# Attention groups of two blocks by four heads, with the results turned in 32x32 blocks on VectorE

## The chip, the cores and the metric

The kernel runs on one core of one Trainium2 chip. The time is device microseconds of one execution of the whole program; the median of a few runs is given. A profiled execution has a span of its own, from its first instruction to its last.

## What is computed

Local attention over 8 sequences of 576 tokens with 8 heads of 64, followed by a gated feed-forward layer over all 4608 tokens. Heads 0 to 3 see the 32 latest tokens ("plain"), heads 4 to 7 see 32 tokens at a distance of four ("strided").

```python
B, H, S, D = q.shape                     # 8, 8, 576, 64
scores = scale * np.matmul(q, k.transpose(0, 1, 3, 2))
mask_plain = (rel >= 0) & (rel < window)                                  # window = 32
mask_dil = (rel >= 0) & (rel < window * dilation) & (rel % dilation == 0) # dilation = 4
masks = np.stack([mask_plain if h < H // 2 else mask_dil for h in range(H)], axis=0)
scores = np.where(masks[None, :, :, :], scores, -1000000000.0)
scores = scores - np.max(scores, axis=-1, keepdims=True)
attn = np.exp(scores)
attn = attn / (np.sum(attn, axis=-1, keepdims=True) + 1e-09)
attn_out = np.matmul(attn, v)
x = np.ascontiguousarray(attn_out.transpose(0, 2, 1, 3)).reshape(B * S, H * D)   # 4608 x 512
g = x @ w_gate                                                            # 512 x 1536
silu = g * (1.0 / (1.0 + np.exp(-g)))
return silu * (x @ w_val) @ w_out                                         # 4608 x 512
```

## The kernel before

**The feed-forward layer sets the frame.** x is kept turned, with its 512 features on partitions (four blocks of 128, NK) and tokens along the free axis. Every fp32 number is split into a high and a low part that TensorE multiplies in one pass each, so a product is three matmuls. The first 1536 tokens go in four chunks of 384 (CH): for each chunk and each of 12 blocks f of the hidden layer, gv_mm issues 12 matmuls into bank_g and 12 into bank_v, and out_mm 12 into bank_o (L459, L496). The other 3072 tokens go in three chunks of 1024 by Strassen's seven products (products, L777, 128x512 each), whose inputs are made from the four quarters x32[a][t] (a: which half of the features, t: which 512 tokens). Weights come in 24 units at the start and pass through ScalarE, VectorE and GpSimd (w_one, stages E, T, B, H, L) before they can be used.

**Attention runs beside it in 46 packs.** In a block, 32 queries meet 64 keys. A pack (class Pack) holds 3 or 4 groups, and a group holds four blocks of 32 queries, one on each quarter of the 128 partitions, for two heads. Before the change a pack belongs to one pair of heads: the pair's two heads lie on the two halves of the rows of q and k (and side by side in the result), and the four quarters hold four blocks of queries, in a strided pack one for each residue modulo four. ORDER (2, 0, 3, 1) is the order of the pairs, and the order of x's feature blocks.

For pack m: scores (L354) multiplies q and k into the PSUM tile `two`; for packs 0 to 7 the mask is added by a matmul ahead, later by VectorE (L366). shift takes the maximum (L368) and subtracts it (L369); exps is the exponential on ScalarE (L374); turn_e turns the weights on TensorE (L378, one transpose of 128x128 per group), keys copies them to SBUF on ScalarE (L384); results multiplies them by v (L394), with a column of ones that gives the sums; norm adds epsilon, inverts and scales on VectorE (L403 to L405) into the buffer y.

y has queries on partitions, and x needs features there. turn_y turns each group of y on TensorE (L412) by one of two identities: a plain one, or one with its columns in another order, which puts strided queries back in the order of tokens. x_copies then takes the result from PSUM: in the chunks of 384 ScalarE makes the high part and VectorE the low part (L429, L430; in the opening L444, L448), later ScalarE copies into x32 (L438).

**What sets the order.** The opening (packs 0 to 3) is written out by hand in a string of steps: Q scores, S shift, X exps, T turn_e, K keys, A results, N norm, U turn_y, H and L the two parts of x, W a stage of the weights, Y idle matmuls. Afterwards a table of visits gives each pack two slots between the matmul groups of the layer: at A(m) the sums of pack m-1, the scores of m, norm of m-1, shift and exps of m; at B(m), three or more slots on, turn_y of m-1, turn_e and keys of m, x_copies of m-1. Within an engine a scheduler places the instructions. `two`, q and k, v, e, y and the turned weights have one buffer each after the opening.

## Time and profile before

| what | value |
|---|---|
| time, median of 3 runs | 947.46 us (946.64 to 948.33) |
| span of the profiled execution | 945.3 us |
| feed-forward matmuls in chunks of 384 | to about 383 us |
| the three chunks of 1024 | 383 to 572, 572 to 759, 759 to 945 us |
| last visit of a pack | about 735 us |

The span of the profiled execution lies 2.2 us below the median of the runs. In the profile PE is TensorE's matmuls, PEld its weight loads, DVE is VectorE, ACT ScalarE, POOL GpSimd, SP SyncE. A row of a group has its line, engine and operation, what it writes and reads, its count, the time during which any of it ran, the mean of one in ns, and the idle time before it. A row in order of time has its start and how long it lasted in us; at its end stands in brackets how long the engine had stood idle and what ended that. Matmuls overlap, so how far one group pushes the next back is read from start to start. A row of the waits has the engine and line that waited, for whom, the sum in us, how often, and the longest. A row of a stretch has its bounds, its length, the busy time of PE, PEld, DVE, ACT and POOL with their counts, the granted clock, the share of the DMA and its GB/s.

### The profile page before, as it was taken

What the parts mean: (1) busy time and instruction counts of PE and PEld (TensorE: products, weight loads), DVE (VectorE), ACT (ScalarE), POOL (GpSimd) and SP (SyncE); (2) the same over time, 40 slices, a digit from 0 to 9 for tenths busy, and PEclk for the clock granted to TensorE, in tenths of its full rate; (3) what the DMA queues carried; (4) which work ended last, traced back from release to release, by engine and by line L of the source; (5) the groups of instructions that cost most, each with busy time, mean ns of one, the idle gap of its engine ahead of it and who ended that gap; (6) DMA issues with size and microseconds to landing.
All of it is one profiled execution on the core that took longest, in us unless ns stands there. A gap on an engine that the chain in (4) does not pass through costs nothing.

```text
span 945.3 us, 21894 instructions
## 1 busy us (share of the span) xinstructions
PE 929.0 (98%) x9193; PEld 810.9 (86%) x9193; DVE 633.3 (67%) x1008; ACT 391.9 (41%) x687; POOL 345.9 (37%) x364
## 2 busy tenths in 40 slices
PE   7899999999999999999999999999999999999998
PEld 4799999999999999888888788888887888888886
DVE  4767566676677865666568984666689845656882
ACT  4885323233233334343344553343355523334352
POOL 0765421111111131224245672232257723344481
PEclk9999999999999999999999999999999999999999
DMA  9985156577767791776667678776764786655573
GB/s 371 330 282 202 36 200 204 189 235 238 237 196 236 244 324 39 226 245 205 227 205 258 202 241 260 229 235 199 254 203 162 232 256 192 198 185 176 177 249 107
DMA packets 75249, 205.25 MB, mean 217 GB/s; under 512 B 7568, under 2 KB 23824, under 8 KB 75152
## 3 DMA queue, kind: packets, MB, share of 16 engines
q0 software_dynamic: 27216, 99.10, 33.4%
q1 hardware_dynamic: 35696, 65.07, 19.3%
q10 hardware_dynamic: 12240, 39.70, 12.7%
q8 instruction: 72, 1.18, 0.5%
q14 instruction: 25, 0.20, 0.1%
HBM read 161.37 MB, written 42.47 MB: 216 GB/s over the span
## 4 chain that ended last, share of the span: by engine, by line
PE 91%; DVE 4%; DMA 2%; ACT 2%; issue 1%; ACTq 0%; DVEq 0%
PE bo L777 30%; PE bg L777 11%; PE bv L777 11%; PE bo L496 10%; PE bv L459 10%; PE bg L459 10%; PE two L394 3%; PE two L354 2%; PE two L378 2%; DVE at_float L740 2%; PE two L412 1%; DMA at_int<-w 1%; DMA at_float<-qkb 1%; ACT at_float32r L274 0%; DVE at_float L805 0%
## 5 line engine op out<-in xcount | busy, mean ns | idle before, releaser
L777 PE MATMUL bo<-at_float32r 128*128 128x512 f32 x1296 | 308.0, 391 | 0.0
L777 PEld LDWEIGHTS bo<-at_float32r 128*128 128x128 f32 x1296 | 242.1, 188 | 51.6 <-ACT at_float L503 0.2
L706 POOL DMA_DIRECT2D at_float32r<-pieces x189 | 103.5, 548 | 249.7 <-PE bo L777 147.0
L740 DVE TENSOR_TENSOR at_float<-bo,at_float 128x512 f32<-128x512 f32 x168 | 113.8, 686 | 109.6 <-ACT at_float L782 59.8
L488 POOL TENSOR_TENSOR at_float32r<-at_float,at_float32r 128x384 fp32r<-128x384 f32 x48 | 55.4, 1154 | 219.7 <-PE bo L496 179.7
L777 PE MATMUL bv<-at_float32r 128*128 128x512 f32 x486 | 129.7, 393 | 0.0
L777 PE MATMUL bg<-at_float32r 128*128 128x512 f32 x486 | 129.6, 393 | 0.0
L740 DVE TENSOR_TENSOR at_float32r<-at_float,at_float32r 128x512 fp32r<-128x512 f32 (+1 forms) x84 | 99.2, 1205 | 40.5 <-ACT at_float32r L767 24.9
L459 PE MATMUL bg<-at_float32r,at_float32r 128*128 128x384 f32 x576 | 110.9, 339 | 2.1 <-DVE at_float L473 1.3
L740 POOL TENSOR_TENSOR at_float32r<-at_float,at_float32r 128x512 fp32r<-128x512 f32 x63 | 96.4, 1532 | 44.7 <-ACT at_float32r L767 43.3
L459 PE MATMUL bv<-at_float32r,at_float32r 128*128 128x384 f32 x576 | 110.6, 339 | 0.0
L496 PE MATMUL bo<-at_float32r,at_float32r 128*128 128x384 f32 x576 | 110.1, 338 | 0.0
L777 PEld LDWEIGHTS bv<-at_float32r 128*128 128x128 f32 x486 | 90.1, 188 | 19.3
L777 PEld LDWEIGHTS bg<-at_float32r 128*128 128x128 f32 x486 | 90.2, 188 | 19.0 <-DVE at_float32r L740 0.2
L767 ACT CAST at_float32r<-at_float 128x512 fp32r<-128x512 f32 x126 | 76.2, 622 | 68.1 <-PE bv L777 23.2
L459 PEld LDWEIGHTS bg<-at_float32r,at_float32r 128*128 128x128 f32 x576 | 100.0, 188 | 3.8 <-POOL at_float32r L278 1.1
L496 PEld LDWEIGHTS bo<-at_float32r,at_float32r 128*128 128x128 f32 x576 | 100.2, 188 | 0.9
L459 PEld LDWEIGHTS bv<-at_float32r,at_float32r 128*128 128x128 f32 x576 | 100.0, 188 | 1.0 <-DVE at_float L478 0.3
L803 ACT ACTIVATE at_float<-at_float 128x512 f32<-128x512 f32 x72 | 45.6, 633 | 85.4 <-DVE at_float L740 85.2
L473 DVE SCALAR_TENSOR_TENSOR at_float<-at_float,bg 128x384 f32<-128x384 f32 x48 | 26.6, 553 | 76.7 <-ACT at_float L468 76.7
L782 ACT COPY at_float<-bg 128x512 f32<-128x512 f32 x63 | 36.9, 586 | 86.2 <-PE bg L777 86.1
L278 POOL TENSOR_TENSOR at_float32r<-at_int,at_float32r 128x768 fp32r<-128x768 f32 x24 | 45.8, 1916 | 41.5 <-ACT at_float32r L274 41.3
(80 smaller groups left out, 966.3 us busy)
## 6 DMA issues: line engine op xcount, KB each, us to landing
at_float32r<-pieces POOLq DMA_DIRECT2D x189, 512.0 KB, 4.5
pieces<-at_float32r SPq DMA_DIRECT2D x126, 256.0 KB, 4.8
at_int<-w SPq DMA_DIRECT2D x24, 768.0 KB, 6.9
at_float<-vb ACTq DMA_DIRECT2D x28, 390.0 KB, 4.6
at_float<-vb ACTq DMA_DIRECT2D x14, 520.0 KB, 5.5
at_float<-qkb ACTq DMA_DIRECT2D x14, 448.0 KB, 5.5
out<-at_float SPq DMA_DIRECT2D x24, 256.0 KB, 5.3
at_float<-qkb ACTq DMA_DIRECT2D x10, 544.0 KB, 6.7
```

The lines of the kernel that those rows point to most:

```text
L278: nc.gpsimd.tensor_tensor(out=lo, in0=wst.pop(u).bitcast(F32), in1=hi, op=ALU.subtract)
L394: nc.tensor.matmul(out=two[BQ * j:BQ * j + BQ, h, (D + 1) * g:(D + 1) * (g + 1)], lhsT=t[r, BQ * i:BQ * i + BQ], rhs=v[r, i, :], start=Tru ...
L459: nc.tensor.matmul(out=bank[:, :CH], lhsT=wcol(f, o, low), rhs=x[ORDER[j]], start=n == 0, stop=n == len(ops) - 1)
L473: last["h"] = nc.vector.scalar_tensor_tensor(out=t, in0=t, scalar=1.0, in1=bank_g[:, :CH], op0=ALU.add, op1=ALU.mult)
L488: nc.gpsimd.tensor_tensor(out=hl, in0=hst[i][0], in1=hst[i][1], op=ALU.subtract)
L496: nc.tensor.matmul(out=bank_o[j][:, :CH], lhsT=wcol(f, 2 * DM + P * j, low), rhs=x, start=f == 0 and low == 0 and x is hh, stop=f == NF - ...
L706: nc.gpsimd.dma_start(out=taken[asked], in_=pieces[asked % NPIECE])
L740: engine.tensor_tensor(out=out, in0=a, in1=b, op=op)
L767: nc.scalar.copy(out=o[:, 0], in_=src)
L777: nc.tensor.matmul(out=bank, lhsT=w, rhs=x, start=first and n == 0 and t in FRESH, stop=last and n == len(ops) - 1, skip_group_check=True)
L782: nc.scalar.copy(out=kept[KEPT[t]][r], in_=banks[0][r][:, :CS])
L803: nc.scalar.activation(out=f, in_=g, func=AF.Tanh, scale=0.5)
```

## The change

A group now holds, for two blocks of queries, all four plain or all four strided heads. The four quarters of the partitions hold the four heads, and the two halves of the rows hold the two blocks (i = 0, 1). A plain pack covers half of its tokens with each half of the rows; a strided pack covers two of the four residues, and a second pack (part) the other two. The count of packs (46) and of groups (152) stays, and so do the shapes of scores, turn_e and results.

With one head on each quarter, turning every 32x32 block of y by itself puts features on partitions and tokens along the free axis: quarter j then holds 32 features of head j, and y's two halves of features (c) lie side by side. turn_y becomes one VectorE transpose of the whole y, in place, or straight into x32 for a plain pack of the last three chunks. One feature block of x now holds half of the features of four heads; the rows of the gate and value weights are laid out to match on the host. x_hi and x_lo are indexed by plain or strided. The copies into x read y in SBUF. The second identity is no longer loaded; the table of masks has 16 groups instead of 12; q and k of plain packs have more columns, since each head's keys lie apart. Strided copies write every fourth column of x32, and each half of it is cleared once on GpSimd.

```diff
 def packs():
-    out = [Pack(c, p, CH * c, CH * c + CH) for c in range(NPLAIN) for p in ORDER]
+    out = []
+    for c in range(NPLAIN):
+        lo = CH * c
+        half = [Pack(c, 0, n, lo + CH // 2 * n, lo + CH // 2 * (n + 1)) for n in range(2)]
+        rest = [Pack(c, 1, n, lo, lo + CH) for n in range(2)]
+        out += half + rest if c == 0 else [rest[0], half[0], rest[1], half[1]]
...
     def norm(m, two, pool):
...
-        nc.vector.tensor_tensor(out=y.rearrange("q g h d -> q h g d"), in0=s[:, :, :, :D],
-                                in1=z.unsqueeze(3).broadcast_to([P, 2, ng, D]), op=ALU.mult)
+        nc.vector.tensor_tensor(out=y.rearrange("q (c i g d) -> q i g c d", c=2, i=2, g=ng),
+                                in0=s[:, :, :, :D].rearrange("q i g (c d) -> q i g c d", c=2),
+                                in1=z.unsqueeze(3).unsqueeze(4).broadcast_to([P, 2, ng, 2, D // 2]), op=ALU.mult)
...
-    def turn_y(m, bank):
-        for g in range(pk(m).ng):
-            nc.tensor.transpose(out=bank[:, P * g:P * g + P], in_=st[m]["y"][:, g].rearrange("q h d -> q (h d)"),
-                                identity=idents[:, pk(m).order])
+    def turn_y(m):
+
+        y = st[m]["y"]
+        out = y
+        if pk(m).chunk >= NPLAIN and not pk(m).strided:
+            t, o = divmod(pk(m).lo - T0 - 2 * CS * (pk(m).chunk - NPLAIN), CS)
+            n = 2 * BQ * pk(m).ng
+            out = x32[1][t][:, :, o:o + n]
+            y = y.rearrange("p (c t) -> p c t", c=2)
+        nc.vector.transpose(out=out, in_=y)
...
+    def x_copy(m, what):
+        c = pk(m).chunk
+        for first, o, n in x_runs(m):
+            src, xh, xl = x_views(m, first - CH * c, o, n, *(t[c % 2][pk(m).strided] for t in (x_hi, x_lo)))
+            if what == "hi":
+                nc.scalar.copy(out=xh, in_=src)
+            else:
+                nc.vector.tensor_tensor(out=xl, in0=src, in1=xh, op=ALU.subtract)
...
+                    if t not in clear:
+                        clear.add(t)
+                        nc.gpsimd.memset(x32[0][t], 0.0)
+                    src, dst = x_views(m, a, o, w, x32[0][t])
+                    nc.scalar.copy(out=dst, in_=src)
...
-        ops = [(j, 0, x) for j in range(NK) for x in (xh, xl)] + [(j, 1, xh) for j in range(NK)]
+        ops = [(j, 0, x) for j in KORDER for x in (xh, xl)] + [(j, 1, xh) for j in KORDER]
...
-        for what in ("Q0 Q1 Y2 S0 X0 T0 Y2 S1 K0 X1 A0 M0 W0 Q2 N0 T1 K1 S2 X2 Q3 W1 W0 S3 X3 A1 U0 N1 W2 T2 K2 H0 L0 W3 W4 "
-                     "T3 A2 K3 W1 U1 N2 A3 H1 L1 W0 W2 U2 N3 W3 H2 U3 L2 W4 H3 L3 W1 W0 W2 W1 W2 W3 W0 W0").split():
+        for what in ("Q0 Q1 Y2 S0 X0 T0 Y2 S1 K0 X1 A0 M0 W0 Q2 N0 T1 K1 S2 X2 Q3 U0 W1 H0 W0 S3 X3 A1 N1 L0 U1 W2 T2 K2 H1 L1 W3 W4 "
+                     "T3 A2 K3 W1 N2 U2 A3 H2 W0 L2 W2 N3 U3 W3 H3 L3 W4 W1 W0 W2 W1 W2 W3 W0 W0").split():
...
             if m < NPK:
                 shift(m, two, later, m < 8)
+            if m > 4:
+                turn_y(m - 1)
+            if m < NPK:
                 exps(m)
...
         elif what == "B":
-            if m > 4:
-                turn_y(m - 1, two[:, 0])
             if m < NPK:
                 turn_e(m, two[:, 1])
                 keys(m, two[:, 1], later)
             if m > 4:
-                x_copies(m - 1, two[:, 0])
+                x_copies(m - 1)
```

KORDER is (2, 3, 0, 1), the plain feature blocks first. Lines of the changed kernel that the rows below name: L388, L390 and L391 are the mask's addition, the maximum and the subtraction (before L366, L368, L369), L425 to L427 are norm (L403 to L405), L444 is the transpose of y, L400 is turn_e (L378), L499 and L536 are the matmuls of gv_mm and out_mm (L459, L496), L780, L845 and L846 are element-wise passes of the chunks of 1024 (L740, L805, L806). at_... are SBUF buffers.

TensorE at slot B of pack 23, in the last chunk of 384, before:

```order
L459 MATMUL bg<-at_384_float32r,at_1536_float32r 128x384 x12
L459 MATMUL bv<-at_384_float32r,at_1536_float32r 128x384 x12
L412 MATMUL two<-at_256_float_59,at_384_float_1071 128x128 x3
L378 MATMUL two<-at_256_float_59,at_512_float_691 128x128 x4
L496 MATMUL bo_490<-at_384_float32r,at_1536_float32r 128x384 x2
```

The same place after:

```order
L499 MATMUL bg<-at_768_float32r,at_1536_float32r 128x384 x12
L499 MATMUL bv<-at_768_float32r,at_1536_float32r 128x384 x12
L400 MATMUL two<-at_128_float_59,at_512_float_675 128x128 x4
L536 MATMUL bo_474<-at_384_float32r,at_1536_float32r 128x384 x2
```

The three turns of pack 22's results are gone from between the matmuls of the layer and turn_e; the rest keeps its order.

VectorE at slot A of pack 23, before:

```order
L403 TENSOR_SCALAR at_6_float_285<-two 128x6
L404 RECIPROCAL at_6_float_285<-at_6_float_285 128x6
L405 TENSOR_TENSOR at_384_float_1071<-two,at_6_float_285 128x2x3x64
L366 TENSOR_TENSOR at_512_float_691<-two,at_448_bfloat_58 128x2x4x64
L368 TENSOR_REDUCE at_8_float_2996<-at_512_float_691 128x8
L369 TENSOR_TENSOR at_512_float_691<-at_512_float_691,at_8_float_2996 128x2x4x64
```

The same place after:

```order
L425 TENSOR_SCALAR at_6_float_277<-two 128x6
L426 RECIPROCAL at_6_float_277<-at_6_float_277 128x6
L427 TENSOR_TENSOR at_384_float_1054<-two,at_6_float_277 128x6x2x32
L388 TENSOR_TENSOR at_512_float_675<-two,at_576_bfloat_58 128x2x4x64
L444 STREAM_TRANSPOSE at_384_float_1054<-at_384_float_1054 128x384
L390 TENSOR_REDUCE at_8_float_2958<-at_512_float_675 128x8
L391 TENSOR_TENSOR at_512_float_675<-at_512_float_675,at_8_float_2958 128x2x4x64
```

The transpose of pack 22's results stands between the mask's addition and the maximum of pack 23, ahead of the subtraction.

VectorE at slot A of pack 35, in the first chunk of 1024, where the scheduler puts passes of the layer in between, before, from the scaling of y to the subtraction:

```order
L405 TENSOR_TENSOR at_384_float_1071<-two,at_6_float_285 128x2x3x64
L366 TENSOR_TENSOR at_512_float_691<-two,at_448_bfloat_58 128x2x4x64
L740 TENSOR_TENSOR at_1024_float32r<-at_512_float_536,at_1024_float32r 128x512
L368 TENSOR_REDUCE at_8_float_2996<-at_512_float_691 128x8
L740 TENSOR_TENSOR at_1024_float32r<-at_512_float_4759,at_1024_float32r 128x512
L369 TENSOR_TENSOR at_512_float_691<-at_512_float_691,at_8_float_2996 128x2x4x64
```

The same place after:

```order
L427 TENSOR_TENSOR at_384_float_1054<-two,at_6_float_277 128x6x2x32
L388 TENSOR_TENSOR at_512_float_675<-two,at_576_bfloat_58 128x2x4x64
L444 STREAM_TRANSPOSE at_384_float_1054<-at_384_float_1054 128x384
L390 TENSOR_REDUCE at_8_float_2958<-at_512_float_675 128x8
L780 TENSOR_TENSOR at_1024_float32r<-at_512_float_520,at_1024_float32r 128x512
L391 TENSOR_TENSOR at_512_float_675<-at_512_float_675,at_8_float_2958 128x2x4x64
```

The transpose comes in, and one of the two passes with two SBUF operands that stood ahead of the subtraction no longer stands there.

More of the change, by code (lines that the diff above doesn't have):

```diff
@@ L434, in x_copies @@
                 first -= T0 + 2 * CS * (c - NPLAIN)
                 while n:
[L436 to L448 removed]
+                    t, a = divmod(first, CS)
```

235 lines of the change are left out of this document (121 added, 114 removed).

## The prediction

> **What bounds the kernel now.** I read the engine table and the granted clock first, then the chain of waits, then the list of who waited for whom, then the order of time around single visits.
>
> ```profile
> span 945.3 us, 21894 instructions
> PE 929.0 (98%) x9193; PEld 810.9 (86%) x9193; DVE 633.3 (67%) x1008; ACT 391.9 (41%) x687; POOL 345.9 (37%) x364
> ...
> PEclk9999999999999999999999999999999999999999
> ...
> PE 91%; DVE 4%; DMA 2%; ACT 2%; issue 1%; ACTq 0%; DVEq 0%
> ```
>
> TensorE is busy for 98% of the span at full granted clock, and the chain that ended last runs over it for 91%. So what is taken off TensorE's own stream is worth its time, as long as nothing that TensorE then waits for comes later. The same chain by line shows what turning the results costs it (the row is cut at the view's width):
>
> ```profile
> by line: PE bo L777 30.2%; PE bg L777 10.9%; PE bv L777 10.7%; PE bo L496 10.4%; PE bv L459 10.3%; PE bg L459 10.1%; PE two L394 2.8%; PE two L354 2.4%; PE two L378 1.6%; DVE at_float L740 1.6%; PE two L412 1.5%; issue 1.0%; DMA at_int<-w 1
> PE two L378 <- ACT at_float L374: 3.6, 3, 1.6
> ```
>
> L412 (turn_y) is 1.5% of 945.3 us, 14.2 us, and all of that line goes. The second row is TensorE's list of waits: the visits' other transpose, L378 (turn_e), waited three times, 3.6 us in all, for ScalarE's exponentials (L374). The change touches exactly that place: it takes work off TensorE just ahead of L378, and puts work on VectorE ahead of the exponentials.
>
> **The change, step by step.**
>
> *TensorE loses the turns of the results.* There are 152 groups of 128 columns before and after, so scores, weighted sums and turn_e keep their counts; only L412 falls away: 140 transposes in the visits, 12 in the opening.
>
> ```profile
> L412 PE MATMUL two<-at_float,at_float 128*128 128x128 f32 x140 | 22.1, 272 | 0.0
> 244.31 2.24 PE L459 MATMUL bv<-at_float32r,at_float32r 128*128 128x384 f32 x12
> 246.39 0.49 PE L412 MATMUL two<-at_float,at_float 128*128 128x128 f32 x3
> 246.72 0.60 PE L378 MATMUL two<-at_float,at_float 128*128 128x128 f32 x4
> ...
> 257.00 2.25 PE L459 MATMUL bg<-at_float32r,at_float32r 128*128 128x384 f32 x12
> 259.08 0.60 PE L412 MATMUL two<-at_float,at_float 128*128 128x128 f32 x4
> 259.52 0.49 PE L378 MATMUL two<-at_float,at_float 128*128 128x128 f32 x3
> ```
>
> The mean of 272 ns and the 22.1 us of the group overlap with neighbours, so I take start to start: three transposes push L378 back by 246.72 - 246.39 = 0.33 us, four by 259.52 - 259.08 = 0.44, 0.11 each. 140 x 0.11 = **15.4 us**. The chain's 14.2 agrees once the two visits below are left out in which L412 only shortened a wait. L378 then follows the matmuls directly, as L412 did.
>
> *VectorE gains 46 transposes.* One per pack, of 384 or 512 columns from SBUF to SBUF. No such operation is in the trace. The nearest rows are the passes of the same size over one operand in SBUF, and above them the pass over two SBUF operands that GpSimd often holds up:
>
> ```profile
> L368 DVE TENSOR_REDUCE at_float<-at_float 128x6 f32<-128x384 f32 x26 | 14.3, 551 | 0.7
> L368 DVE TENSOR_REDUCE at_float<-at_float 128x8 f32<-128x512 f32 x12 | 8.2, 683 | 0.3
> L740 DVE TENSOR_TENSOR at_float32r<-at_float,at_float32r 128x512 fp32r<-128x512 f32 x63 | 71.0, 1148 | 24.9 <-ACT at_float32r L767 24.9
> ```
>
> I bound the price between nothing (where the queue has a gap before the next operation anyway) and 1.15 us, and take the rows it is nearest to, one operand and as many columns: 0.55 us for 384 and 0.69 for 512, some 27 us over a queue that has 945 - 633 = 312 us free. What counts is its place: the order of VectorE shows it in every visit between the mask's addition (or the maximum) and the last subtraction, so it stands ahead of the exponentials, and what is queued behind it there is the maximum, the subtraction, then ScalarE's exponentials and TensorE's L378. Each visit's exponentials come later by the transpose of the pack before, d, and TensorE arrives earlier by the turns it no longer does, u (0.33 or 0.44). With s the spare time of before (start of L378 less the end of the exponentials, less the 0.05 us from 521.93 to 521.98 in a visit that waited), d + u - s is given back where it is positive. The rows of the visits with the least to spare, and of the first with enough:
>
> ```profile
> 76.26 0.63 ACT L374 ACTIVATE at_float<-at_float 128x512 f32<-128x512 f32 x1 [0.58 <-DVE at_float L369]
> 77.35 0.60 PE L378 MATMUL two<-at_float,at_float 128*128 128x128 f32 x4
> ...
> 92.07 0.53 ACT L374 ACTIVATE at_float<-at_float 128x384 f32<-128x384 f32 x1
> 92.66 0.54 PE L378 MATMUL two<-at_float,at_float 128*128 128x128 f32 x3
> ...
> 321.02 0.63 ACT L374 ACTIVATE at_float<-at_float 128x512 f32<-128x512 f32 x1 [3.50 <-DVE at_float L369]
> 322.38 0.60 PE L378 MATMUL two<-at_float,at_float 128*128 128x128 f32 x4
> ...
> 344.19 0.64 ACT L374 ACTIVATE at_float<-at_float 128x512 f32<-128x512 f32 x1 [2.58 <-DVE at_float L369]
> 345.71 0.60 PE L378 MATMUL two<-at_float,at_float 128*128 128x128 f32 x4
> ...
> 521.30 0.63 ACT L374 ACTIVATE at_float<-at_float 128x512 f32<-128x512 f32 x1 [2.87 <-DVE at_float L369]
> 521.98 0.66 PE L378 MATMUL two<-at_float,at_float 128*128 128x128 f32 x4 [1.62 <-ACT at_float L374]
> ...
> 538.43 0.53 ACT L374 ACTIVATE at_float<-at_float 128x384 f32<-128x384 f32 x1 [3.93 <-DVE at_float L369]
> 539.56 0.49 PE L378 MATMUL two<-at_float,at_float 128*128 128x128 f32 x3
> ...
> 717.76 0.66 PE L378 MATMUL two<-at_float,at_float 128*128 128x128 f32 x4 [1.16 <-ACT at_float L374]
> ...
> 196.84 0.52 ACT L374 ACTIVATE at_float<-at_float 128x384 f32<-128x384 f32 x1
> 199.01 0.49 PE L378 MATMUL two<-at_float,at_float 128*128 128x128 f32 x3
> ```
>
> Pack 6 (77.35): s = 77.35 - 76.89 - 0.05 = 0.41, so 0.55 + 0.33 - 0.41 = 0.47 us. Pack 7 (92.66): s = 0.01, 0.69 + 0.44 - 0.01 = 1.12. Pack 23 (322.38): s = 0.68, 0.20. Pack 25 (345.71): s = 0.83, 0.05. Pack 36 (539.56): s = 0.55, 0.69 + 0.44 - 0.55 = 0.58. Packs 35 (521.98) and 45 (717.76) waited already, s = 0: 0.88 each. Pack 13 (199.01) has 1.60, more than 0.88, and so have the other visits behind the opening (pack 4 has no results to turn). Together **4.2 us given back**. With a transpose at nothing it is still 1.1 (packs 7, 35, 45); at 1.15 us (and 1.53 for 512 columns) the same seven visits give 8.9. At packs 35 and 45 the estimate is loosest: the chain to the subtraction is stretched there by passes between two SBUF operands, and the new order has one of those fewer ahead of the subtraction.
>
> ```profile
> 517.49 2.55 POOL L740 TENSOR_TENSOR at_float32r<-at_float,at_float32r 128x512 fp32r<-128x512 f32 x2
> 518.00 2.59 DVE L740 TENSOR_TENSOR at_float32r<-at_float,at_float32r 128x512 fp32r<-128x512 f32 x1
> ```
>
> Such a pass takes 2.59 us while GpSimd works on the same kind. The Trainium skill, SBUF — State Buffer, section "Who interferes with whom", says that a VectorE instruction with two SBUF inputs contends with GpSimd's reads and one with a single input does not; this pair of rows agrees with the first half, and no row of before shows the second. By that rule the transpose is never held, and the price stays near 0.55 beside GpSimd too.
>
> *Copies of x.* They now read y in SBUF. On ScalarE the plain packs of the last three chunks lose theirs (the transpose writes x directly), the strided packs of chunk 1 get two instead of one. On VectorE the 18 subtractions for the low part get two SBUF operands, so one may rise from about 0.55 towards 2.59 us. They stand behind the exponentials, where TensorE has no wait in the list, and the visits of those chunks after pack 7 have at least 1.6 us: 0, and at most 1. Two clears of 128x1024 on GpSimd come ahead of low-part passes for the second product, which follow several matmul groups later: 0. y has one buffer, and the next visit's scaling must now wait for ScalarE's copy rather than for TensorE's turn; the copy is queued at B, before the next visit's sums that precede the scaling: 0.
>
> *The opening.* It is run by loads and ScalarE, not by TensorE:
>
> ```profile
> 0.00:28.00 28.00, 20.94 (x455) 14.15 (x455) 15.06 (x33) 14.41 (x25) 3.69 (x6) 0.94 0.96 375
> 16.49 0.92 ACT L235 ACTIVATE at_int<-at_int 128x768 f32<-128x768 f32 x1 [2.07 <-DMA at_int<-w]
> ```
>
> TensorE is busy 21 of the first 28 us, so its 12 turns bring nothing, and VectorE (15 of 28) holds four more passes of 0.55. The DMA is 96% busy at 375 GB/s; ahead of the second weight unit, for which ScalarE waits at 16.49, stand 96 KB more (96 columns more of q and k, 48 KB, for each of packs 1 and 3; 64 KB more of masks, 64 KB less of identities): 98304 bytes at 375 GB/s, 0.26 us. The first gate matmuls now need both plain packs, but the last of them still follow pack 3's results. I take **0.3 us lost**, between 1 gained and 1.5 lost.
>
> **The sum:** 945.3 - 15.4 + 4.2 + 0.3 = 934.4 us of span. The median shown is 947.46, 2.2 above the profiled span; I let those 2.2 stand for what lies around it: **936.6 us**.
>
> The Trainium skill speaks against this price: VectorE: DVE Perf Modes, section "The three transpose paths", gives 311 ns for a VectorE transpose of 128x128 in bf16, which read as 128 columns is an estimate of 0.93 us for 384; the visits would give back 7.2 us and the sum would be 939.6. No run here shows it yet.
>
> **The rivals.**
>
> *The transpose costs about twice the row I took.* For: nothing in the trace shows such an operation, so the upper row is as open as the lower. Against: the upper row owes its length to GpSimd, and the passes over one operand agree among themselves (551 and 683 ns). At 1.15 us: 945.3 - 15.4 + 8.9 + 0.3 + 2.2 = 941.3.
>
> *Nothing is given back.* The order after is the scheduler's, and at packs 35 and 45 it drops a pass that could be held 2.59 us. Then the old waits shrink as much as packs 6, 7 and 36 lose: 945.3 - 15.4 + 0.3 + 2.2 = 932.4.
>
> *The time isn't recovered, because every L378 waits for its exponentials.* Each turn's 0.11 us would become a wait: 947.5. Against it stand three waits in 46 visits.
>
> *Slower: VectorE's queue becomes the bound of every visit.* With the same subtraction over all 42 visits, 14 of them wait once the transpose takes 1.75 us, and they give back 15.1, which is the point of no gain; at 2.0 us it is 19.3, and the time 945.3 - 15.4 + 19.3 + 0.3 + 2.2 = 951.7. For: a held pass took 2.59 us. Against: three times the price of the nearest row, for one operand.
>
> **How the numbers follow.** Forecast 0.62, twice the price 0.16, nothing given back 0.09, time not recovered 0.05, slower 0.08. The range goes from 932 (nothing given back) to 942.5 (twice the price, and 1.2 us more in the opening). A measurement of this kernel can tell 0.2%, 1.9 us, from no change: faster 0.62 + 0.16 + 0.09 = 0.87, same 0.05, slower 0.08.
>
> **What would show it.** Right: no transposes of y on TensorE and L378 right behind the matmuls; transposes on VectorE near 550 and 690 ns; TensorE's waits for the exponentials at some 3.6 + 4.2 = 8 us, seven times, at packs 6, 7, 35, 36 and 45 above all; matmul groups as long as before; the first 28 us within 1.5. Wrong: transposes over 1.1 us; waits for exponentials in many visits; TensorE waiting for copies of x, for low parts or for weights, which it doesn't now.

## The result, and the profile after

| kernel | median, us | lowest to highest | ratio to before, 95% |
|---|---|---|---|
| before (4 runs) | 947.6 | 946.64 to 948.33 | |
| changed (4 runs) | 937.27 | 935.84 to 937.64 | 0.9891 [0.9877, 0.9905] |

The change makes the kernel 1.1% faster, 10.3 us. The profiled execution has a span of 934.1 us, 11.2 less than before. Its engine table and, behind the dots, the chain that ended last by engine:

```profile
span 934.1 us, 21615 instructions
...
PE 913.8 (98%) x9041; PEld 795.7 (85%) x9041; DVE 661.9 (71%) x1056; ACT 393.5 (42%) x671; POOL 337.8 (36%) x366
...
PE 90%; DVE 6%; DMA 2%; ACT 2%; issue 1%; SPq 0%; ACTq 0%; DVEq 0%
```

TensorE loses 15.2 us of busy time and 152 matmuls; VectorE gains 28.6 us and stays free for 29% of the span. The chain is still TensorE's, but VectorE's share of it went from 4 to 6%. The groups by line and shape give the price of the new operation (busy time of the group, then the mean of one in ns):

```profile
L444 DVE STREAM_TRANSPOSE at_float<-at_float 128x384 f32<-128x384 f32 x32 | 18.2, 568 | 0.1
L444 DVE STREAM_TRANSPOSE at_float<-at_float 128x512 f32<-128x512 f32 x14 | 9.8, 701 | 0.0
```

Three rows of TensorE's list of waits (line, what it waited for, total, times, longest) hold most of what is given back of the turns:

```profile
PE two L400 <- ACT at_float L396: 4.4, 4, 2.5
PE fs L400 <- ACT at_float L396: 3.2, 1, 3.2
PE bv L499 <- ACT at_float32r L290: 2.7, 1, 2.7
```

The first row is the visits (L400 is turn_e, L396 the exponentials): 4.4 us where before had 3.6. The second is the opening's last pack, the third is new: TensorE waits for the high part of a weight unit (L290). By visit, the waits for exponentials, read from the order of time:

| pack | 4 | 25 | 35 | 36 | 45 | 6, 7, 23 |
|---|---|---|---|---|---|---|
| before, us | 0.78 | 0 | 1.62 | 0 | 1.16 | 0 |
| after, us | 0 | 1.27 | 0.33 | 2.53 | 0.32 | 0 |

Where the 11.2 us arise is seen by comparing when the same matmul of the layer starts (start after less start before; n counts the layer's matmuls ahead of it):

| n, layer matmuls ahead (start before) | 70 (38.3) | 144 (55.5) | 936 (215.1) | 1512 (335.6) | 1584 (351.7) | 2268 (522.4) | 2376 (549.5) | last (940.9) |
|---|---|---|---|---|---|---|---|---|
| difference, us | +2.8 | +1.8 | -2.0 | -5.6 | -3.9 | -8.9 | -6.6 | -11.2 |

The opening loses 2.8 us by matmul 70, and 1.0 of them is back by matmul 144, mostly pack 4's wait of 0.78 us, which is gone. From there each visit gains 0.327 us (three turns) or 0.437 (four), and two places give back: the visit of pack 25 (between matmuls 1512 and 1584) and that of pack 36 (2268 to 2376). These are the two visits in the order of time, VectorE's rows ahead of TensorE's L400:

```profile
337.85 0.80 ACT L487 COPY at_float<-at_float 128x64 f32<-128x64 f32 x2 [3.27 <-DVE at_float L444]
338.45 0.52 ACT L508 ACTIVATE at_float<-bg 128x384 f32<-128x384 f32 x1
338.68 1.23 DVE L780 TENSOR_TENSOR at_float<-at_float,at_float 128x1024 f32<-128x1024 f32 x1 [0.30 <-ACT at_float L487]
339.83 0.68 DVE L391 TENSOR_TENSOR at_float<-at_float,at_float 128x512 f32<-128x512 f32 x1
...
341.57 0.66 PE L400 MATMUL two<-at_float,at_float 128*128 128x128 f32 x4 [1.27 <-ACT at_float L396]
...
529.98 0.70 DVE L444 STREAM_TRANSPOSE at_float<-at_float 128x512 f32<-128x512 f32 x1
530.61 0.51 DVE L390 TENSOR_REDUCE at_float<-at_float 128x6 f32<-128x384 f32 x1
531.04 0.68 DVE L780 TENSOR_TENSOR at_float<-bo,at_float 128x512 f32<-128x512 f32 x1
531.64 0.55 DVE L391 TENSOR_TENSOR at_float<-at_float,at_float 128x384 f32<-128x384 f32 x1
...
532.85 0.55 PE L400 MATMUL two<-at_float,at_float 128*128 128x128 f32 x3 [2.53 <-ACT at_float L396]
```

At pack 25 a sum of the layer (L780) stands ahead of the subtraction (L391) and itself waits 0.30 us for ScalarE's copy of x (L487). At pack 36 the transpose is one of several passes between 528.5 us, when the sums of the pack before begin, and the subtraction.

In the opening the second weight unit comes late. VectorE, ScalarE and TensorE after:

```profile
21.23 0.58 DVE L444 STREAM_TRANSPOSE at_float<-at_float 128x384 f32<-128x384 f32 x1
21.85 0.89 ACT L466 CAST at_float32r<-at_float 128x384 fp32r<-128x384 f32 x1 [0.62 <-DVE at_float L444]
22.77 0.85 DVE L468 TENSOR_TENSOR at_float32r<-at_float,at_float32r 128x384 fp32r<-128x384 f32 x1 [0.96 <-ACT at_float32r L466]
23.54 0.95 DVE L279 SCALAR_TENSOR_TENSOR at_int<-at_int 128x768 int32<-128x768 int32 x1
24.52 0.83 ACT L290 CAST at_float32r<-at_int 128x768 fp32r<-128x768 f32 x1 [1.09 <-DVE at_int L279]
25.40 1.18 PE L499 MATMUL bv<-at_float32r,at_float32r 128*128 128x384 f32 x4 [2.74 <-ACT at_float32r L290]
```

and the same place before (the cast is L444 there, the low part L448, the unit's bits L263, its high part L274; by the order of the steps, cast and low part are pack 1's here and pack 2's above):

```profile
20.79 0.48 ACT L444 CAST at_float32r<-fx 128x384 fp32r<-128x384 f32 x1 [0.29 <-PE fx L412]
21.30 0.56 DVE L448 TENSOR_TENSOR at_float32r<-fx,at_float32r 128x384 fp32r<-128x384 f32 x1 [0.35 <-ACT at_float32r L444]
...
21.77 0.95 DVE L263 SCALAR_TENSOR_TENSOR at_int<-at_int 128x768 int32<-128x768 int32 x1
...
22.75 0.83 ACT L274 CAST at_float32r<-at_int 128x768 fp32r<-128x768 f32 x1 [0.65 <-DVE at_int L263]
```

After, the unit's bits stand in VectorE's queue behind pack 2's low part, that waits for the cast, and that for the transpose. The transpose is new (0.58), and cast and low part take 0.89 and 0.85 us instead of 0.48 and 0.56: together 1.3 us of the 1.77 by which the high part is late. Before, only pack 1's results stood there. That the new order of steps puts pack 2's ahead of the bits is a cause beside the longer passes; the experiments that move the bits forward, below, bear on it.

### The profile page after: what moved, and what is told of

Read it like the earlier page. It is cut to its first block, busy times and chain, and to the rows that moved or that the text cites. A ratio compares the mean times of both kernels' runs of the same rounds, so it can differ in the third digit from the quotient of the medians.

```text
span 934.1 us, 21615 instructions
## 1 busy us (share of the span) xinstructions
PE 913.8 (98%) x9041; PEld 795.7 (85%) x9041; DVE 661.9 (71%) x1056; ACT 393.5 (42%) x671; POOL 337.8 (36%) x366
## 3 DMA queue, kind: packets, MB, share of 16 engines
q8 instruction: 71, 1.16, 0.5%
## 4 chain that ended last, share of the span: by engine, by line
PE 90%; DVE 6%; DMA 2%; ACT 2%; issue 1%; SPq 0%; ACTq 0%; DVEq 0%
PE bo L817 30%; PE bg L817 11%; PE bo L536 11%; PE bv L817 11%; PE bg L499 10%; PE bv L499 10%; PE two L416 3%; PE two L372 3%; DVE at_float L780 2%; PE two L400 2%; DMA at_int<-w 1%; DVE at_float32r L780 1%; DMA at_float<-vb 1%; DVE at_float L391 0%; DVE at_float L845 0%
## 5 line engine op out<-in xcount | busy, mean ns | idle before, releaser
L780 DVE TENSOR_TENSOR at_float<-bo,at_float 128x512 f32<-128x512 f32 x168 | 113.6, 687 | 102.0 <-ACT at_float L822 56.4
L780 DVE TENSOR_TENSOR at_float32r<-at_float,at_float32r 128x512 fp32r<-128x512 f32 (+1 forms) x84 | 99.9, 1213 | 30.9 <-ACT at_float32r L807 19.1
L499 PE MATMUL bg<-at_float32r,at_float32r 128*128 128x384 f32 x576 | 112.0, 342 | 1.7 <-DVE at_float L513 1.7
L499 PE MATMUL bv<-at_float32r,at_float32r 128*128 128x384 f32 x576 | 110.2, 340 | 2.7 <-ACT at_float32r L290 2.7
L536 PE MATMUL bo<-at_float32r,at_float32r 128*128 128x384 f32 x576 | 110.0, 339 | 0.0
L780 POOL TENSOR_TENSOR at_float32r<-at_float,at_float32r 128x512 fp32r<-128x512 f32 x63 | 89.3, 1419 | 53.4 <-ACT at_float32r L807 52.7
L817 PEld LDWEIGHTS bv<-at_float32r 128*128 128x128 f32 x486 | 90.3, 188 | 19.2
L499 PEld LDWEIGHTS bg<-at_float32r,at_float32r 128*128 128x128 f32 x576 | 101.2, 190 | 3.7 <-DVE at_float L513 2.0
L499 PEld LDWEIGHTS bv<-at_float32r,at_float32r 128*128 128x128 f32 x576 | 99.9, 189 | 3.7 <-ACT at_float32r L290 3.0
L536 PEld LDWEIGHTS bo<-at_float32r,at_float32r 128*128 128x128 f32 x576 | 100.4, 188 | 0.8
```

What stands on the lines that cost most here:

```text
L499: nc.tensor.matmul(out=bank[:, :CH], lhsT=wcol(f, o, low), rhs=x[1 - j // 2][:, j % 2], start=n == 0, stop=n == len(ops) - 1)
L536: nc.tensor.matmul(out=bank_o[j][:, :CH], lhsT=wcol(f, 2 * DM + P * j, low), rhs=x, start=f == 0 and low == 0 and x is hh, stop=f == NF - ...
L780: engine.tensor_tensor(out=out, in0=a, in1=b, op=op)
L817: nc.tensor.matmul(out=bank, lhsT=w, rhs=x, start=first and n == 0 and t in FRESH, stop=last and n == len(ops) - 1, skip_group_check=True)
```

## The experiments

My theory after the result: the turns are worth their time, and what is given back depends on the place of single instructions in the queues of VectorE and ScalarE. The rivals: the transposes' own time on VectorE is what is given back; or the opening's clock or loads set the loss. The runs were made in four groups, each beside runs of the kernel before: its medians were 947.58 (the first four experiments told here), 947.55 (the repeat of the changed kernel, idle matmuls, casts in runs, late visits), 947.63 (no late turns, four visits, four visits and opening) and 947.41 us (six visits).

**Without any turn, in the kernel before.** The turns of packs 4 to 45 are left out, nothing takes their place (x is not turned).

```diff
-        for g in range(pk(m).ng):
+        for g in () if m >= 4 else range(pk(m).ng):
```

> The kernel before, with the TensorE turns of the results left out from pack 4 on and nothing in their place (x is then made of unturned sums, so the output is not the reference's). Theory A, the turns cost TensorE 0.109 us each and nothing hides them: 140 x 0.109 = 15.3 us less, of which packs 7, 35 and 45 take back 0.43 + 0.33 + 0.33 because turn_e there waits for the exponentials anyway: 14.2 us less than before, a ratio of 0.985. Rival, the turns lie beside other work: within 3 us of before.

935.71 us (934.78 to 938.44), ratio 0.9881 [0.9862, 0.9899]: 11.9 us less, 12.3 by the profiled spans. The expectation of 14.2 is missed by some 2 us, mostly by pack 36, which was not expected to wait. TensorE then waits at packs 6, 23, 35, 36 and 45 for 0.25, 0.26, 0.64, 2.55 and 0.62 us, 4.3 us together (2.8 before, without pack 4), and in the changed kernel for 4.45. **So as much is given back in the visits without a single transpose on VectorE**: from matmul 144 on this kernel gains 11.9 us, the changed one 13.0. Visit by visit only pack 36's wait is the same. Pack 25's 1.27 us arises in the changed kernel alone, and the small ones are larger here.

What pack 36 waits for can be read from VectorE's queue. Between pack 35's subtraction and the sums with which pack 36's chain begins VectorE has 15 passes in 13.4 us before, 17 in 16.2 us in the changed kernel and 16 in 16.3 us here, all of them passes of the layer and none a transpose. Pack 36's chain therefore begins 2.8 us later against pack 35's, and TensorE itself is only 0.3 us faster from the one visit to the other. Once the turns are gone the scheduler orders the layer's passes in another way; why it does so wasn't looked into.

**Three transposes instead of one** (from pack 4 on; three times in place turn the blocks as once).

```diff
-        nc.vector.transpose(out=out, in_=y)
+        for _ in range(3 if m >= 4 else 1):
+            nc.vector.transpose(out=out, in_=y)
```

> The changed kernel with each transpose of y from pack 4 on done three times (two of the three stand ahead of the subtraction). Theory A, only visits with less to spare than the transpose takes pay: one more transpose ahead of the exponentials, 0.57 or 0.70 us, costs 0.42 at pack 7, 0.27 at 22, 0.57 at 25, 0.57 at 35, 0.70 at 36, 0.57 at 45: 3.1 us more than the changed kernel. Rival B, VectorE is near its limit in every visit: two more transposes in 42 visits, 50 us of VectorE time, cost over 10 us. Rival C, the transposes are covered entirely: under 0.5 us.

945.09 us (941.55 to 946.42), ratio 0.997 [0.996, 0.9981]. Between the expectations: 7.8 us more than the changed kernel. Four visits wait, packs 6, 7, 25 and 36, for 2.69, 0.54, 2.42 and 4.41 us. At packs 5 to 7 only one of the three transposes stands ahead of the subtraction, as in the changed kernel, and from pack 8 on two of them. So pack 6, with 0.67 us to spare in the changed kernel, should not have waited. Its rows show why it does:

```profile
80.72 0.91 ACT L251 ACTIVATE at_int<-at_int 128x768 f32<-128x768 f32 x1 [2.63 <-DMA at_int<-w]
81.52 0.61 ACT L396 ACTIVATE at_float<-at_float 128x512 f32<-128x512 f32 x1
...
82.19 0.66 PE L400 MATMUL two<-at_float,at_float 128*128 128x128 f32 x4 [2.69 <-ACT at_float L396]
```

The exponentials stand in ScalarE's queue behind the first pass over a weight unit (L251), which waits 2.63 us for its load; what ends TensorE's wait there is that load. At packs 25 and 36 the longer queue of VectorE adds 1.2 and 1.9 us, and behind pack 36's wait the granted clock stands at 0.50 for 3.4 us.

**The transpose behind the subtraction.**

```diff
-        nc.vector.tensor_tensor(out=ev, in0=s, in1=mx.unsqueeze(3).broadcast_to([P, 2, ng, BK]), op=ALU.subtract)
+        last["s"] = nc.vector.tensor_tensor(out=ev, in0=s, in1=mx.unsqueeze(3).broadcast_to([P, 2, ng, BK]), op=ALU.subtract)
...
-                turn_y(m - 1)
+                with tc.issue_after(last["s"].ins):
+                    turn_y(m - 1)
```

> The changed kernel, with the VectorE transpose of y issued behind the subtraction of the next pack, no longer ahead of it. Theory A, the new waits at packs 25, 35, 36 and 45 (1.27, 0.33, 2.53, 0.32 us) come from the transpose ahead of the exponentials: those of 25 and 36 shrink by 0.57 and 0.70, the small ones vanish, 1.9 us less than the changed kernel in all. Rival B, they come from VectorE's own backlog and from other passes that the order puts ahead of the subtraction: less than 0.5 us of change, the wait of pack 36 stays near 2.5.

941.2 us (938.05 to 941.91), ratio 0.9927 [0.9908, 0.9947]: 4 us more than the changed kernel, where 1.9 less was expected. Packs 7, 25, 35, 36 and 45 wait for 2.14, 0.84, 1.12, 2.37 and 1.15 us, 7.6 together. Pack 36 still waits 2.37 us with the transpose out of the way. VectorE's rows ahead of it show why:

```profile
532.17 0.16 DVE L425 TENSOR_SCALAR at_float<-two 128x8 f32<-128x8 f32 x1
...
533.67 0.68 DVE L781 TENSOR_TENSOR at_float<-bo,at_float 128x512 f32<-128x512 f32 x1
534.27 0.54 DVE L390 TENSOR_REDUCE at_float<-at_float 128x6 f32<-128x384 f32 x1
534.73 0.68 DVE L781 TENSOR_TENSOR at_float<-bo,at_float 128x512 f32<-128x512 f32 x1
535.33 0.55 DVE L391 TENSOR_TENSOR at_float<-at_float,at_float 128x384 f32<-128x384 f32 x1
535.79 0.70 DVE L444 STREAM_TRANSPOSE at_float<-at_float 128x512 f32<-128x512 f32 x1
536.55 0.55 PE L400 MATMUL two<-at_float,at_float 128*128 128x128 f32 x3 [2.37 <-ACT at_float L396]
```

Where the transpose stood, ahead of the maximum (L390), the scheduler has put a pass of the layer (L781) that is as long. From the sums of the pack before (532.17) to L400 it takes 4.38 us here, 4.37 in the changed kernel (528.48 to 532.85), and 4.38 in the kernel without any turn. The place of the transpose was expected to set the wait at pack 36; it doesn't.

**The opening in another order.**

```diff
-  ... A3 H2 W0 L2 W2 N3 U3 W3 H3 L3 W4 ...
+  ... A3 H2 W2 N3 U3 W3 H3 W0 L2 L3 W4 ...
```

> The changed kernel, in whose written opening the second weight unit's bits, pack 3's scaling, its transpose and its high part stand ahead of pack 2's low part. Theory A, the opening loses its 2 us because VectorE waits there for ScalarE's high part of pack 2 while the weight unit stands behind it: TensorE's 2.7 us wait for the weights' high part falls below 1.3 us, and the first gate matmuls end about 1.5 us earlier; 1 to 1.5 us less in all. Rival, the loads set the opening: within 0.3 us of the changed kernel.

943.02 us (939.67 to 944.75), ratio 0.9943 [0.9921, 0.9964]. The wait for the unit fell from 2.7 to 0.9 us as expected, but the first pass over unit 2 (W0), now behind pack 3's cast, started 2.3 us later; pack 4 then waits 2.1 us, pack 25 3.48. The high part of unit 1 starts at 22.50, even ahead of the 22.75 of the kernel before, and yet matmul 144 is 5.0 us behind the kernel before instead of 1.8.

**The changed kernel again.**

> The changed kernel once more, beside the three below, to see how its waits and its opening vary from one execution to another. Its first profile had TensorE waits for exponentials of 4.4 and 3.2 us and a granted clock of 0.50 in two stretches of the opening, 18.7 to 22.6 us and 26 to 29.3 us. If both are fixed by the order of the instructions: 937.3 us within 1, the same two stretches, the same visits waiting. If they hang on chance in the DMA and in the clock: the second profile shows other stretches or other visits, and single runs spread by 3 us or more.

936.26 us (935.92 to 938.03), ratio 0.9886 [0.9871, 0.9901]. The same visits wait, each within 0.02 us of the first profile, and the layer's matmuls start within 0.5 us of it. In these two executions the waits don't hang on chance. Only the granted clock of the opening differs: 0.50 from 20.0 to 30.2 us in one stretch, where the first profile has 19.2 to 22.6 and 26.0 to 29.4.

**Idle matmuls in the opening's wait,** nine of 512 columns over the mask constants, into a bank that nothing uses at that time, behind pack 3's results (step Z).

```diff
-  ... A3 H2 W0 L2 W2 ...
+  ... A3 Z9 H2 W0 L2 W2 ...
```

> The changed kernel with nine matmuls of 512 columns into an unused bank behind pack 3's results in the opening, where TensorE stands for 2.74 us (22.7 to 25.4) until the second weight unit is there. Theory: the granted clock of 0.50 from 26 to 29.3 us follows from that idle stretch; kept busy until some 24.6 us, TensorE runs the first 16 gate and value matmuls at full speed, and the opening is 1.3 to 1.8 us shorter: about 935.7. Rival: the clock falls for another reason (the load of the 32x32 matmuls before, or chance): the stretch stays at 0.50 and the time within 0.5 of the changed kernel, or it is slower by what the nine matmuls delay.

936.39 us (935.24 to 940.13), ratio 0.9879 [0.9863, 0.9896], no difference from the repeat. The profiled execution is the longest one, 940.13. By stretches (busy time of each engine, then TensorE's granted clock) the changed kernel:

```profile
24.00:26.00 2.00, 0.60 (x3) 0.60 (x4) 1.89 (x5) 0.83 (x1) 0.57 (x1) 1.00 1.02 411
26.00:28.00 2.00, 2.00 (x8) 0.78 (x6) 1.05 (x2) 1.98 (x3) 1.17 (x1) 0.50 0.99 399
28.00:30.00 2.00, 2.00 (x8) 2.00 (x9) 1.97 (x3) 1.62 (x3) 0.28 (x1) 0.65 0.26 92
```

and with the idle matmuls:

```profile
20.00:24.00 4.00, 3.67 (x96) 2.67 (x81) 2.41 (x7) 3.07 (x5) 1.74 (x1) 0.50 1.03 419
24.00:26.00 2.00, 1.98 (x9) 0.72 (x8) 1.90 (x6) 0.83 (x1) 0.12 (x1) 0.89 0.99 406
26.00:28.00 2.00, 1.64 (x8) 0.92 (x8) 1.05 (x2) 1.53 (x3) 1.62 (x1) 1.00 0.93 369
28.00:30.00 2.00, 1.62 (x10) 1.60 (x10) 2.00 (x3) 1.60 (x4) 0.00 (x0) 1.00 0.29 120
34.00:38.00 4.00, 4.00 (x17) 4.00 (x16) 3.25 (x4) 3.15 (x5) 2.53 (x3) 0.59 0.87 305
```

From 24.4 to 34.7 us the clock is full, but it stands at 0.50 from 14.2 to 24.4 and again from 34.7 to 38.1, 13.7 us in all against 6.8. One execution can't show that the idle matmuls hold it, and its matmul 144 is 3.8 us behind the kernel before, not 1.8. What the full clock from 26 to 30 us shows is that TensorE then waits for the next units instead: it is busy 1.6 of each 2 us.

That the clock sets little of the opening's loss is seen in the kernels with the changed kernel's opening. Where it stands at 0.50 for 6.8 us there, matmul 144 is 1.8 and 2.4 us behind the kernel before (first profile, three transposes); for 10.2 us, 1.8 and 2.0 (repeat, four visits); for 17.1 us, 2.0, 2.0 and 2.6 (late transposes, six visits, all late visits).

**Casts of the opening in runs.** The strided packs' casts of x in the first chunk write neighbouring columns instead of every fourth (the tokens of that chunk then stand in another order).

```diff
-                *(t[:, :, first:first + n].rearrange("p c (u r) -> p c r u", r=DIL)[:, :, r:r + 2] for t in x))
+                *(t[:, :, first:first + n].rearrange("p c (u r) -> p c r u" if pk(m).chunk else "p c (r u) -> p c r u",
+                                                     r=DIL)[:, :, r:r + 2] for t in x))
```

> The changed kernel with the strided packs' casts of x in the opening written in runs of neighbouring columns instead of every fourth pair (the rows of x then stand in another order and the output of that chunk is not the reference's). Theory: these casts and their low parts take 0.89 us where plain ones take 0.51 to 0.55, because they write every fourth column; that is 0.7 us of the 2.74 us that TensorE waits for the second weight unit at 25.4 us, and with it goes a part of the half-speed stretch behind it. Casts at about 0.52, low parts at 0.56, the wait at 2 us or less, the time 1 to 2.5 us below the changed kernel. Rival: the time lies in the reading (y is read in pieces too) or in the loads: casts stay at 0.89 us, or the wait stays at 2.7 us and the time within 0.7.

The rows of pack 2 and of the unit (one line further down in this kernel):

```profile
21.85 0.51 ACT L467 CAST at_float32r<-at_float 128x384 fp32r<-128x384 f32 x1 [0.28 <-DVE at_float L444]
22.39 0.56 DVE L469 TENSOR_TENSOR at_float32r<-at_float,at_float32r 128x384 fp32r<-128x384 f32 x1 [0.58 <-ACT at_float32r L467]
...
23.85 0.83 ACT L290 CAST at_float32r<-at_int 128x768 fp32r<-128x768 f32 x1 [0.68 <-DVE at_int L279]
```

Cast and low part fall to 0.51 and 0.56, the unit's high part comes 0.67 us earlier, the wait is 1.8 us, and matmul 144 starts 0.96 us earlier. As expected in the opening; but the median is 937.32 us (936.74 to 940.04), ratio 0.9899 [0.9884, 0.9914], no gain on the changed kernel's 937.27 and 936.26. In the profiled execution, the longest, pack 7 waits 1.61 us for its exponentials and pack 25 2.14 instead of 1.27, behind packs 25 and 36 the clock stands at 0.50 for 3.4 us each, and the gain is gone.

**Without the opening's late transposes** (packs 2 and 3 stay unturned).

```diff
-  ... N2 U2 A3 ... N3 U3 W3 ...
+  ... N2 A3 ... N3 W3 ...
```

> The changed kernel without the transposes of packs 2 and 3 in the opening (their results stay unturned, so the output is not the reference's). Theory: of the 1.8 us that the opening loses against the kernel before, 1.0 came back when the casts of these packs were written in runs; the other part is the two transposes of 0.57 us in VectorE's queue ahead of unit 1's and unit 2's bits: unit 1's high part about 0.6 us earlier (23.9), unit 2's about 1.1 (27.7), the layer's 144th matmul 0.6 to 1.2 us earlier, and the time 936 or a little less. Rival: they lie beside the loads and ScalarE: the high parts start where they did, the 144th matmul too.

941.24 us (940.59 to 943.12), ratio 0.9937 [0.9924, 0.9951]. The expected gain didn't come: the high part of unit 1 starts at 24.37, 0.15 us earlier. From pack 2's norm (L425 at 20.66, in the changed kernel at 20.22) to that high part it takes 3.71 us instead of 4.30, shorter by the one transpose, but the norm itself is 0.44 later. Pack 4 then waits 1.9 us and pack 7 1.39, and the kernel is 5 us slower than the repeat. Of the opening's loss the part of the strided writes is shown; the transposes' part is only seen in this interval.

**The second half of late visits moved back.** If TensorE arrives too early, it should do other matmuls first.

```diff
-        visits(m, a, a + 3)
+        visits(m, a, a + 3 + (m >= 24))
...
-        visits(m, a, a + 6)
+        visits(m, a, a + 8)
```

> The changed kernel with the second half of a visit (the turn of the exponentials) two slots later in the two chunks of 1024 columns that have visits of six slots, and one slot later for packs 24 to 26. Theory: at packs 25, 35, 36 and 45 TensorE waits 1.27, 0.33, 2.53 and 0.32 us for the exponentials only because it arrives too early; two slots are some 2 us and more, so nearly all of these 4.45 us go: 4 us below the changed kernel, about 933. Rival: the wait moves to the next results or to the products that read the copies of x, which stand closer behind now: within 1 us of the changed kernel, with new TensorE waits for copies of the keys or of x.

936.86 us (936.09 to 937.69), ratio 0.9889 [0.9874, 0.9903]. The rival's case: no visit waits for exponentials, but TensorE waits for the copies of the keys (L406):

```profile
PE two L416 <- ACT at_float L406: 3.9, 2, 2.0
```

Both are the results that follow packs 35 and 45, where the second half now stands directly ahead of the next visit.

**Only four visits moved,** packs 25, 35 and 45 by one slot, 36 by two.

```diff
-        visits(m, a, a + 3)
+        visits(m, a, a + 3 + (m == 25))
...
-        visits(m, a, a + 6)
+        visits(m, a, a + 6 + (n == 8) + 2 * (n == 9))
```

> The changed kernel with the second half of the visit moved at four packs alone: 25, 35 and 45 one slot later, 36 two. Theory: the 3.9 us that the kernel with all late visits moved waited for copies of keys arose only at packs 35 and 45, whose keys then stood directly ahead of the next results; with one slot there instead of two these waits go, and the waits for exponentials at 25, 35, 36 and 45 (1.27, 0.33, 2.53, 0.32 us) go as before: 3 to 4.4 us below the changed kernel, about 933. Rival: one slot is too little for the one or too much for the other at 35 and 45, and half is given back: 935.

931.41 us (930.64 to 935.5), ratio 0.9837 [0.9818, 0.9857], 4.9 us below the repeat of the changed kernel, somewhat more than expected. Of the four waits 0.29 us is left, at pack 36. The profiled execution is the longest one, 935.5; in it pack 7 waits. ScalarE's and TensorE's rows there:

```profile
94.19 0.88 ACT L251 ACTIVATE at_int<-at_int 128x768 f32<-128x768 f32 x1 [2.86 <-DMA at_int<-w]
...
95.29 0.52 ACT L396 ACTIVATE at_float<-at_float 128x384 f32<-128x384 f32 x1
...
95.86 0.55 PE L400 MATMUL two<-at_float,at_float 128*128 128x128 f32 x3 [2.26 <-ACT at_float L396]
```

It is the mechanism of pack 6 above: the exponentials behind a weight unit's first pass, and that behind its load. In the changed kernel's profile the same pass started at 91.20 us, in time. The stretch costs 4.0 us against the changed kernel though the wait is 2.26, since the clock falls behind it:

```profile
92.00:95.00 3.00, 1.60 (x10) 1.28 (x8) 2.35 (x4) 0.81 (x2) 1.17 (x1) 1.00 0.94 363
95.00:98.00 3.00, 2.14 (x11) 2.14 (x12) 1.59 (x2) 3.00 (x8) 1.02 (x1) 0.83 0.19 70
98.00:101.00 3.00, 3.00 (x13) 3.00 (x12) 2.50 (x4) 0.84 (x4) 1.74 (x1) 0.61 0.00 0
```

**The four visits and the opening.** As above, and in the opening the bits of units 1 and 2 ahead of the low parts, the shift of unit 2 ahead of pack 3's cast.

```diff
-  ... A3 H2 W0 L2 W2 N3 U3 W3 H3 L3 W4 W1 W0 W2 W1 W2 ...
+  ... A3 H2 W0 W2 L2 N3 U3 W3 W4 W1 H3 W2 L3 W0 W1 W2 ...
```

> The same four slots, and in the opening the bits of weight units 1 and 2 ahead of the low parts of packs 2 and 3 on VectorE, and the shift of unit 2 ahead of pack 3's cast on ScalarE. Theory: the opening is set by the units' conversion, in whose queues the transposes and the long strided casts stand: the high part of unit 1 starts at 24.5 us in the changed kernel and at 22.75 before. With its bits first it starts about 23.5, unit 2's about 27.2 instead of 28.8, and the opening gains 1 to 1.5 us on top of the slots: about 931.5. Rival: the low parts are late instead, and the scheduler's new order behind the opening costs more than it gains, as in the kernel whose opening was reordered first: 934 or above.

931.74 us (931.57 to 932.62), ratio 0.9834 [0.9821, 0.9847]. Unit 1's high part starts at 23.53 and unit 2's at 27.03, as expected, and matmul 70 is 1.5 us behind the kernel before instead of 2.8; but pack 4 then waits 1.7 us, and at matmul 144 nothing is left of it (+2.5). So 931.5 was met by the four slots alone, not by the opening.

**Six visits moved.** The four, and packs 6 and 7 by one slot.

```diff
-        visits(4 + n, 5 + 13 * n // 2, 8 + 13 * n // 2)
+        visits(4 + n, 5 + 13 * n // 2, 8 + 13 * n // 2 + (n in (2, 3)))
```

> The four moved slots, and packs 6 and 7 turn their exponentials one slot (twelve matmuls, some 2 us) later as well; on TensorE nothing else changes. Theory: the profiled execution of the four slots alone was slow by some 4 us (935.5 us against 930.6 to 931.9) because the exponentials of pack 7 stood in ScalarE's queue behind a weight unit's first pass, which waited 2.86 us for its load, and TensorE, having stood for 2.26 us, ran at a lower granted clock until 101 us. One slot later covers that: no wait at packs 6 and 7 in any execution, all runs between 930 and 932, the median about 930.8. Rival: the slow run had another cause (the clock in the opening, or chance): single runs still reach 934 to 935.5.

**930.66 us (930.41 to 931.16, 5 runs), ratio 0.9824 [0.981, 0.9837].** It beats both kernels, and its five runs lie within 0.75 us. In its list of TensorE's waits the visits have one row:

```profile
PE two L400 <- ACT at_float L396: 0.3, 1, 0.3
```

In the profiled execution no wait is left at packs 6 and 7, as expected. The time is 6.6 us below the changed kernel's first median and 5.6 below the repeat's, for other numbers in the table of visits.

## Why the prediction was right

The time was forecast at 936.6 us and is 937.27, inside the range. Its steps:

**The turns, 15.4 us: right.** Neighbouring layer matmuls around a visit come 0.327 us (three turns) and 0.437 us (four) closer together, 0.109 each, 15.3 for the 140. Start to start was the right measure.

**The transpose at 0.55 and 0.69 us: right,** with 0.568 and 0.701 measured. The nearest rows were passes of one operand over as many columns. The transposes are never held up by GpSimd: 19 of the 46 run beside one of its element-wise passes, and the longest of all takes 0.704. So the rival of twice the price falls. The estimate of 0.93 us from the Trainium skill, VectorE: DVE Perf Modes, section "The three transpose paths", is refuted for fp32 of 384 columns, while SBUF — State Buffer, section "Who interferes with whom", by which an instruction with at most one SBUF input isn't held outside the two-port modes, agrees with these times.

**Given back at the visits, 4.2 us: the size is wrong and so is its cause.** Measured from matmul 144 on: pack 25 +1.49, 36 +2.75, 35 -1.30, 45 -0.84, packs 6, 7 and 23 nothing; **+2.1 together** (25 and 36 cost 0.22 each more than their waits). TensorE's waits for exponentials came to 4.4 us at four visits, not to 8 at seven. The failed step is "d + u - s is given back", which took s, the spare time of before, as fixed and added the transpose d to the way from the sums to the exponentials. That way, and the time from the sums to TensorE's arrival at turn_e, were (us, before to after):

| pack | 6 | 7 | 23 | 25 | 35 | 36 | 45 |
|---|---|---|---|---|---|---|---|
| sums to end of exponentials | 2.97 to 3.30 | 2.74 to 3.27 | 3.69 to 4.02 | 4.80 to 5.76 | 8.59 to 7.08 | 4.32 to 4.32 | 8.12 to 7.07 |
| sums to TensorE's arrival | 3.42 to 3.97 | 2.80 to 3.60 | 4.42 to 4.70 | 5.69 to 4.55 | 7.02 to 6.80 | 4.92 to 1.84 | 7.02 to 6.80 |

At packs 6, 7 and 23 the transpose does lengthen the way, but VectorE also begins the sums earlier against TensorE, and no wait comes of it. At packs 35 and 45 one pass of the layer fewer stands in the way, and it is shorter in spite of the transpose. At pack 36 the way is as long as before, with the transpose in the place of a pass, and what changes is the arrival: 2.8 of the 3.1 us are the layer's passes that VectorE now has between packs 35 and 36, 0.3 TensorE's own gain. At pack 25 a pass of the layer stands ahead of the subtraction; with that pass behind it, in the kernel with the late transposes, pack 25 still waits 0.84 us, and what holds it there stays open. So at pack 36, which gives back most, it is the new order of the layer's passes, more than u or d; with no transpose at all the visits wait 4.3 us against 4.45. With two transposes ahead of the subtraction the wait grows at packs 25 and 36.

**The opening, 0.3 us lost: mis-sized, and outside its bounds of 1 gained to 1.5 lost; it is 1.8 us by matmul 144.** The text named ScalarE and the loads as its bound and put VectorE's extra passes into free time. But the units' bits pass through the same queue, and with the bits ahead in it unit 1's high part starts at 22.50 instead of 24.52, so the loads didn't hold it. It missed that a strided pack's cast now writes every fourth column itself, where TensorE's turn used to put the columns in order: 0.89 us for 0.48; written in runs, the opening gains 0.96 us. What remains, the transpose ahead of the cast and the new order of the steps, is not settled by the runs: with the bits of the units moved forward matmul 70 gains 1.3 us, and nothing of it is left at matmul 144.

**The copies of x at 0: nearly right.** TensorE never waits for them, but VectorE's sum at pack 25 waits 0.30 us for one.

**The sum** was 945.3 - 15.4 + 4.2 + 0.3 = 934.4; measured 945.3 - 15.3 + 2.1 + 1.8 = 933.9, 0.2 below the span of 934.1. Two terms were off by 2.1 and 1.5 us in opposite directions, so that the total came out better than its parts is luck.

The slower rival didn't occur. The kernel with three transposes per visit doesn't reach its point of no gain (1.75 us ahead of the exponentials): two of the three stand there from pack 8 on, 1.1 us for 384 columns, and the kernel is at 945.09 us, still below before. For 1.15 us the prediction's sum gives 941.3; of the 3.8 us above it pack 6's wait for the load is 2.7 in the profiled execution.

## What to carry to other kernels

When work leaves the bounding engine, its stations move forward against the other engines: after such a change, look again at the table that says when the dependent matmuls stand in its stream, and at what the scheduler has moved; here the table brought another 5.6 us beside the change's 10.3. An engine that serves both a tight chain and passes behind loads lets the chain wait for a load: count what may stand ahead in its queue, not only durations. A layout that saves a reordering pays for it where the data is written with a stride.

## What the runs showed of the hardware

- **Writing every fourth column costs** 0.89 us for 0.51 on ScalarE, and 0.85 for 0.56 on VectorE, which reads one operand so too, 128x384 fp32. The Trainium skill, SBUF — State Buffer, section "Door 1: The DMA port swizzle", says that SBUF has lines of 16 bytes and each access that crosses to a new one pays. Four fp32 apart, every one does, and the runs agree in sign; the page gives no figure for it. It also names 4 fp32 as how far one can stride for free, and here a step of four was not free.
- **The granted clock can fall to half after short pauses.** At pack 7 of the kernel with four moved visits TensorE stood for 2.26 us, and 3.4 us at 0.50 followed; with nearly the same wait there (2.14 us) the kernel with the late transposes stayed at 1.00. Behind the opening the fourteen profiled executions have 19 pauses of TensorE of 1.96 us or more, and 9 of them were followed by 3.41 us at 0.50, among them both that were longer than 3.41 us (3.48 and 4.41); the clock fell behind no shorter pause. In the openings the stretches at 0.50 last 3.4, 6.8, 10.2 or 17.1 us. The Trainium skill, TensorE: Matmul & The Clock Gate, section "What's actually happening", has windows of about 3.4 us that run freely of the kernel; that fits the lengths and the chance, but here pauses shorter than a window were enough.
- **The spread of single runs.** The changed kernel spread over 2.2 us (eight runs), the four moved visits over 4.9 (four runs), the six over 0.75 (five runs). In the longest run of the four moved visits the cause is the late load at pack 7; that slack in the queues makes a kernel steadier in general is not shown by so few runs.
